# Attention and gated FFN on one core: two stages one after the other, and a woven layout with block transposes and column tiles

## The chip, the cores and the metric

One core of a Trainium2 chip runs one program. The metric is device time in microseconds (us). The kernel before was timed in three runs: 223.93, 224.61 and 225.66 us, median 224.61.

## The reference

q, k and v have the shape (batch 4, heads 4, tokens 1088, 32), in float32. S1 and S2 are 8 x 32.

```
phi(x)[i,j] = (S1 x)[i] * (S2 x)[j]              # 64 features of one token and head
kv  = sum over tokens of phi(k) (outer) v        # 64 x 32 for each batch and head
z   = sum over tokens of phi(k)                  # 64
att = phi(q) kv / (phi(q) . z + 1e-6)            # 32 for each token and head
x   = att, heads side by side                    # 4352 tokens x 128
out = (relu(x w_gate) * (x w_val)) w_out         # 128 -> 1536 -> 128
```

The order of work is set by the data: kv and z of a batch need all its keys, the attention of a token needs kv and z, and the FFN of a token needs its attention.

## The kernel before, in words

**Attention** goes through the four batches in a Python loop. The tokens of a batch are cut into eight chunks of 128 and one of 64, with a token on each partition. SyncE loads k and q, one DMA for each head plus one for the last 64 tokens, in runs of 128 bytes (32 floats); GpSimd loads v and casts it to 16 bits. For each chunk of k, TensorE transposes it (L135), VectorE copies the result from PSUM (L137), TensorE multiplies by s_bd, which holds S1 and S2 four times on the diagonal (L140), ScalarE copies (L142), GpSimd forms the outer products kp (L154), and TensorE adds kv (L158) and zbig, from which z comes (L144). After the nine chunks ScalarE places kv and z into two block matrices, kv_bd and the third part of s_bd_ext. The nine chunks of q then go the same way (transpose L183, matmul L188, outer product qp L195), and further: TensorE transposes qp (L202), VectorE copies (L208), TensorE multiplies by kv_bd (L211), GpSimd and VectorE form the denominator (L215 to L225), VectorE divides (L228), TensorE transposes the quotient (L236) and ScalarE writes it into xT, 128 features x 4352 tokens, 16 bits (L237).

**The FFN** starts when the attention's PSUM pools are closed: eight chunks of 512 tokens and one of 256. In a chunk each of the twelve slices j of the hidden width takes a matmul with w_gate (L250, g_ps), a relu on ScalarE (L252, g_sb), a matmul with w_val (L255, v_ps), and their product on VectorE (L256, ht); twelve accumulating matmuls with w_out follow (L260, ot_ps). ScalarE copies (L263), TensorE transposes four blocks (L272), ScalarE scales (L273), SyncE stores.

Every engine works through its own list in order. The lists are made by a list scheduler, which takes the instructions as the code issues them and orders them by its own costs and the free buffers of the pools; it can look ahead, so k of a batch overlaps with q of the batch before.

Of the kernel before, what the change touches and what calls it, by code (L numbers as in the profile page):

```python
# [9 lines left out]
BF16 = mybir.dt.bfloat16  # L11
FP16 = mybir.dt.float16
ALU = mybir.AluOpType
ACTF = mybir.ActivationFunctionType
XSCALE = 1.0 / 16.0


@with_exitstack
def kernel(
# [12 lines left out]
    nc = tc.nc  # L32
# [5 lines left out]
    NTOK = B * S  # L38
# [4 lines left out]
    SC = 128  # L43
    NCH = (S + SC - 1) // SC
    csz = [min(SC, S - i * SC) for i in range(NCH)]
    NFULL = S // SC
    CLAST = S - NFULL * SC
    HR = H * R

    const = ctx.enter_context(tc.tile_pool(name="const", bufs=1))  # L50
    xpool = ctx.enter_context(tc.tile_pool(name="xpool", bufs=1))
    a_in = ctx.enter_context(tc.tile_pool(name="a_in", bufs=2))
    a_tr = ctx.enter_context(tc.tile_pool(name="a_tr", bufs=5))
    a_ab = ctx.enter_context(tc.tile_pool(name="a_ab", bufs=5))
    a_kp = ctx.enter_context(tc.tile_pool(name="a_kp", bufs=5))
    a_qpt = ctx.enter_context(tc.tile_pool(name="a_qpt", bufs=5))
    a_sm = ctx.enter_context(tc.tile_pool(name="a_sm", bufs=6))
    a_pb = ctx.enter_context(tc.tile_pool(name="a_pb", bufs=2))
    f_h = ctx.enter_context(tc.tile_pool(name="f_h", bufs=2))
    f_g = ctx.enter_context(tc.tile_pool(name="f_g", bufs=4))  # L60
    f_o = ctx.enter_context(tc.tile_pool(name="f_o", bufs=4))


    ident = const.tile([128, 128], FP32)
    make_identity(nc, ident)
    ident16 = const.tile([128, 128], FP16)
    make_identity(nc, ident16)

    s_bd = const.tile([HD, 2 * HR], FP32)
    nc.vector.memset(s_bd, 0.0)  # L70
    for h in range(H):
        nc.scalar.dma_start(out=s_bd[h * D:(h + 1) * D, h * R:(h + 1) * R],
                            in_=S1.transpose([1, 0]))
        nc.scalar.dma_start(out=s_bd[h * D:(h + 1) * D, HR + h * R:HR + (h + 1) * R],
                            in_=S2.transpose([1, 0]))

    s1f = const.tile([HR, HD], FP32)
    nc.vector.memset(s1f, 0.0)
    for h in range(H):
        nc.scalar.dma_start(out=s1f[h * R:(h + 1) * R, h * D:(h + 1) * D], in_=S1)  # L80

    wg_sb = const.tile([DM, NJ, 128], FP16)
    nc.gpsimd.dma_start(out=wg_sb, in_=moe_w_gate.rearrange("m (j f) -> m j f", j=NJ))
    wv_sb = const.tile([DM, NJ, 128], FP16)
    nc.gpsimd.dma_start(out=wv_sb, in_=moe_w_val.rearrange("m (j f) -> m j f", j=NJ))
    wo_sb = const.tile([128, NJ, DM], FP16)
    nc.gpsimd.dma_start(out=wo_sb, in_=moe_w_out.rearrange("(j f) m -> f j m", f=128))

    xT = xpool.tile([HD, NTOK], FP16)

    with tc.tile_pool(name="ps_tr", bufs=2, space=bass.MemoryType.PSUM) as ps_tr, \
         tc.tile_pool(name="ps_xt", bufs=1, space=bass.MemoryType.PSUM) as ps_xt, \
         tc.tile_pool(name="ps_ab", bufs=1, space=bass.MemoryType.PSUM) as ps_ab, \
         tc.tile_pool(name="ps_kv0", bufs=1, space=bass.MemoryType.PSUM) as ps_kv0, \
         tc.tile_pool(name="ps_kv1", bufs=1, space=bass.MemoryType.PSUM) as ps_kv1, \
         tc.tile_pool(name="ps_zb", bufs=1, space=bass.MemoryType.PSUM) as ps_zb, \
         tc.tile_pool(name="ps_nd", bufs=1, space=bass.MemoryType.PSUM) as ps_nd:
        ab2_ps = ps_ab.tile([SC, 2, 96], FP32, name="ab2_ps")
        ndq2_ps = ps_nd.tile([SC, 512], FP32, name="ndq2_ps")
        xtsz_ps = ps_xt.tile([HD, 96], FP32, name="xtsz_ps")  # L100

        for b in range(B):
            q4 = a_in.tile([SC, NCH, H, D], FP32, name="q4")
            k4 = a_in.tile([SC, NCH, H, D], FP32, name="k4")
            v4 = a_in.tile([SC, NCH, H, D], FP16, name="v4")

            def load_qkv(dst, src, eng):
                for h in range(H):
                    eng.dma_start(
                        out=dst[:, 0:NFULL, h],  # L110
                        in_=src[b, h, 0:NFULL * SC, :].rearrange("(c p) d -> p c d", p=SC),
                    )
                eng.dma_start(
                    out=dst[:CLAST, NFULL],
                    in_=src[b, :, NFULL * SC:, :].transpose([1, 0, 2]),
                )

            load_qkv(k4, k, nc.sync)
            load_qkv(q4, q, nc.sync)
            load_qkv(v4, v, nc.gpsimd)  # L120

            kv_ps = [ps_kv0.tile([128, 2 * D], FP32, name="kv0_ps"),
                     ps_kv1.tile([128, 2 * D], FP32, name="kv1_ps")]
            zbig_ps = ps_zb.tile([HR, HR], FP32, name="zbig_ps")
            kv_bd = a_pb.tile([128, 2, F], FP16, name="kv_bd")
            s_bd_ext = a_pb.tile([HD, 3 * HR], FP32, name="s_bd_ext")
            zbig_sb = a_pb.tile([HR, HR], FP32, name="zbig_sb")

# [180 lines left out]
```

## Time and profile before

| what | value |
|---|---|
| median of three runs | 224.61 us (223.93 to 225.66) |
| span of the profiled execution, first to last instruction | 223.3 us |
| TensorE (PE) busy | 179.1 us, 80% |
| VectorE (DVE) busy | 106.2 us, 48% |
| ScalarE (ACT) busy | 103.2 us, 46% |
| GpSimd (POOL) busy | 82.1 us, 37% |
| first matmul of the attention | 14.2 us |
| first FFN matmul on the chain that ended last | 144.2 us |

The profiled execution's own time is known by its span alone: what lies around the first and the last instruction is not in the page, and the median of the runs is 1.3 us above that span. In the page, an engine's busy time is the union of its instructions. Matmuls are pipelined, so two matmuls that start 0.2 us apart may each be shown as 0.4 us long; the distance between their starts tells the pace. PEld is the loading of a matmul's stationary operand.

### The profile page before, as it was taken

The numbers are of one execution on the slowest core, as the hardware profiler recorded it, in microseconds if no ns is written. First come the engines' busy times: TensorE is split into PE (matmuls) and PEld (weight loads), VectorE is DVE, ScalarE is ACT, GpSimd is POOL, SyncE is SP. The second block draws the span as 40 slices with busy tenths as digits, with TensorE's granted clock in tenths as the row PEclk, the third lists the DMA queues.
The fourth block names the chain that finished last, engine by engine and source line by source line (L and its number), as shares of the span: only waits on it lengthen the run. The fifth ranks groups of instructions, "written<-read, shape, count | busy, mean of one in ns | idle before, by whom it ended". The sixth has DMA issues, their size and how long they took to land.

```text
span 223.3 us, 3087 instructions
## 1 busy us (share of the span) xinstructions
PE 179.1 (80%) x906; PEld 105.7 (47%) x906; DVE 106.2 (48%) x290; ACT 103.2 (46%) x307; POOL 82.1 (37%) x187
## 2 busy tenths in 40 slices
PE   0018999659949989689997795599999999999992
PEld 0005666437727667366674552234444444444460
DVE  0002003333114431224422154369998989989981
ACT  0021243112433213332234362158898988988981
POOL 8402578997378853158632385000000000000000
PEclk9999999999999999999999999559999999999998
DMA  7999989765494100000000000000110110110110
GB/s 95 156 125 135 156 107 84 72 23 44 72 52 72 28 0 0 3 0 1 0 1 3 0 0 1 0 0 3 47 48 0 47 51 0 47 42 6 50 47 23
DMA packets 61776, 9.18 MB, mean 41 GB/s; under 512 B 57152, under 2 KB 61504, under 8 KB 61760
## 3 DMA queue, kind: packets, MB, share of 16 engines
q1 hardware_dynamic: 39952, 6.69, 17.8%
q0 software_dynamic: 19568, 2.30, 17.0%
q10 hardware_dynamic: 2240, 0.01, 0.7%
q8 instruction: 7, 0.11, 0.2%
q14 instruction: 9, 0.07, 0.1%
HBM read 9.06 MB, written 2.23 MB: 51 GB/s over the span
## 4 chain that ended last, share of the span: by engine, by line
PE 60%; POOL 18%; DMA 7%; issue 5%; DVE 4%; ACT 4%; SPq 0%; ACTq 0%; POOLq 0%
PE v_ps L255 12%; PE ot_ps L260 10%; PE g_ps L250 10%; POOL qp L195 8%; PE ab_ps L140 7%; DMA k<-in_k_dram 4%; PE zbig_ps L144 4%; POOL den L223 3%; POOL bw L215 3%; PE tr_ps L183 3%; PE kv_ps L158 2%; DMA s_bd<-in_S_dram 2%; PE xtsz_ps L236 2%; PE ndq_ps L211 2%; PE ab_ps L188 2%
## 5 line engine op out<-in xcount | busy, mean ns | idle before, releaser
L256 DVE TENSOR_TENSOR ht<-g_sb,v_ps 128x512 f16<-128x512 f16 (+1 forms) x108 | 67.3, 656 | 8.1 <-PE v_ps L255 4.0
L252 ACT ACTIVATE g_sb<-g_ps 128x512 f16<-128x512 f32 (+1 forms) x108 | 59.1, 583 | 11.5 <-PE g_ps L250 7.9
L255 PE MATMUL v_ps<-xT,wv_sb 128*128 128x512 f16 (+1 forms) x108 | 40.7, 379 | 0.8 <-DVE ht L256 0.4
L250 PE MATMUL g_ps<-xT,wg_sb 128*128 128x512 f16 (+1 forms) x108 | 40.9, 382 | 0.0
L260 PE MATMUL ot_ps<-ht,wo_sb 128*128 128x512 f16 (+1 forms) x108 | 39.8, 374 | 0.2 <-DVE ht L256 0.2
L154 POOL TENSOR_TENSOR kp<-ab_sb 128x256 f16<-128x256 f32 (+1 forms) x36 | 22.2, 623 | 23.8 <-ACT ab_sb L142 20.6
L135 PE MATMUL tr_ps<-ident,k 128*128 128x128 f32 (+1 forms) x36 | 14.7, 435 | 17.8 <-DMA k<-in_k_dram 14.2
L188 PE MATMUL ab_ps<-s_bd_ext,tr_sb 128*128 128x96 f32 (+1 forms) x72 | 25.3, 455 | 4.5 <-ACT s_bd_ext L175 2.6
L195 POOL TENSOR_TENSOR qp<-ab_sb 128x256 f16<-128x256 f32 (+1 forms) x36 | 22.5, 625 | 13.1 <-ACT ab_sb L190 12.3
L142 ACT COPY ab_sb<-ab_ps 128x64 f32<-128x64 f32 (+1 forms) x36 | 7.6, 211 | 41.0 <-PE ab_ps L140 31.8
L140 PE MATMUL ab_ps<-s_bd,tr_sb 128*128 128x64 f32 (+1 forms) x72 | 23.5, 431 | 2.3 <-DMA s_bd<-in_S_dram 2.3
L188 PEld LDWEIGHTS ab_ps<-s_bd_ext,tr_sb 128*128 128x128 f32 (+1 forms) x72 | 17.1, 298 | 9.6 <-ACT ab_sb L190 5.4
L137 DVE COPY tr_sb<-tr_ps 128x128 f32<-128x128 f32 (+1 forms) x36 | 9.6, 275 | 25.4 <-PE tr_ps L135 21.9
L222 DVE TENSOR_REDUCE den<-bw 128x4 f32<-128x32 f32 (+1 forms) x36 | 6.6, 184 | 30.6 <-POOL bw L215 30.3
L190 ACT COPY ab_sb<-ab_ps 128x96 f32<-128x96 f32 (+1 forms) x36 | 8.6, 238 | 25.7 <-PE ab_ps L188 22.4
L140 PEld LDWEIGHTS ab_ps<-s_bd,tr_sb 128*128 128x128 f32 (+1 forms) x72 | 17.5, 305 | 4.7 <-issue 3.1
L208 DVE COPY qpt<-ndq_ps 128x256 f16<-128x256 f16 (+1 forms) x36 | 10.0, 277 | 17.8 <-PE ndq_ps L202 17.2
L135 PEld LDWEIGHTS tr_ps<-ident,k 128*128 128x128 f32 (+1 forms) x36 | 8.0, 229 | 20.9 <-issue 14.4
L250 PEld LDWEIGHTS <-wg_sb 128*128 128x128 f16 x108 | 11.1, 103 | 13.2 <-issue 4.7
L260 PEld LDWEIGHTS <-wo_sb 128*128 128x128 f16 x108 | 10.6, 98 | 14.1 <-issue 3.8
L255 PEld LDWEIGHTS <-wv_sb 128*128 128x128 f16 x108 | 10.7, 99 | 12.6 <-issue 2.9
L237 ACT COPY xT<-xtsz_ps 128x128 f16<-128x128 f16 (+1 forms) x36 | 9.4, 261 | 14.8 <-PE xtsz_ps L236 14.7
(44 smaller groups left out, 207.5 us busy)
## 6 DMA issues: line engine op xcount, KB each, us to landing
k<-in_k_dram SPq DMA_DIRECT2D x16, 128.0 KB, 3.5
q<-in_q_dram SPq DMA_DIRECT2D x16, 128.0 KB, 4.6
out_dram<-o_sb SPq DMA_DIRECT2D x8, 256.0 KB, 2.3
v<-in_v_dram POOLq DMA_DIRECT2D x16, 64.0 KB, 3.4
wg_sb<-in_moe_w_gate_dram POOLq DMA_DIRECT2D x1, 384.0 KB, 5.9
wv_sb<-in_moe_w_val_dram POOLq DMA_DIRECT2D x1, 384.0 KB, 7.5
wo_sb<-in_moe_w_out_dram POOLq DMA_DIRECT2D x1, 384.0 KB, 11.0
s_bd<-in_S_dram ACTq DMA_DIRECT2D x8, 1.0 KB, 5.6
```

Source lines behind the costliest of these rows:

```text
L135: nc.tensor.transpose(tr_ps[:, :c], k4[:c, ci].rearrange("s h d -> s (h d)"), ident[:c, :c])
L137: nc.vector.tensor_copy(out=tr_sb[:, :c], in_=tr_ps[:, :c])
L140: nc.tensor.matmul(ab_ps[:c, 0:2 * HR], tr_sb[:, :c], s_bd, start=True, stop=True)
L154: nc.gpsimd.tensor_tensor(out=kp[:c], in0=a_bc, in1=b_bc, op=ALU.mult)
L188: nc.tensor.matmul(ab_ps[:c], tr_sb[:, :c], s_bd_ext, start=True, stop=True)
L195: nc.gpsimd.tensor_tensor(out=qp[:c], in0=a_bc, in1=b_bc, op=ALU.mult)
L208: nc.vector.tensor_copy(out=qpt[:, :, :c], in_=qpt_ps[:, :, :c])
L250: nc.tensor.matmul(g_ps[:, :cs], wg_sb[:, j], xT[:, c0:c0 + cs], start=True, stop=True)
L252: nc.scalar.activation(out=g_sb[:, :cs], in_=g_ps[:, :cs], func=ACTF.Relu)
L255: nc.tensor.matmul(v_ps[:, :cs], wv_sb[:, j], xT[:, c0:c0 + cs], start=True, stop=True)
L256: nc.vector.tensor_tensor(out=ht[:, j, :cs], in0=g_sb[:, :cs], in1=v_ps[:, :cs], op=ALU.mult)
L260: nc.tensor.matmul(ot_ps[:, :cs], wo_sb[:, j], ht[:, j, :cs], start=(j == 0), stop=(j == NJ - 1))
```

## The change

The kernel function is written anew; the arithmetic stays the same, with the division moved from the quotient to one factor of phi(q).

- **Layout.** k and q are loaded so that partition 32h + t holds head h, and each run in memory is eight tokens of one head, 1 KB. v is loaded in runs of 1 KB too. VectorE transposes k and q in 32 x 32 blocks from SBUF to SBUF (kT, qT), in three pieces each for a batch.
- **Column tiles.** The matmuls by S1 and S2 have s_bd, 128 x 32 for each, as the stationary operand, and four groups of 32 tokens times 4 columns go to four quadrants of the output's partitions. VectorE turns the result back in 32 x 32 blocks (kab, qab).
- **Fewer, larger steps.** Outer products are made for two token columns at a time (512 elements per partition), the denominator for 512 tokens at a time, and the numerator comes out of TensorE already with the features on the partitions, so it is copied into xT with no transpose. The last 64 tokens of all four batches form one group, "rest".
- **Woven order.** A table gives each step a slot; a slot is one slice j of an FFN chunk. The table's order is the order in which the code issues the steps. Batch 0's attention comes first. Attention of batch b lies beside the two FFN chunks of batch b - 1 (chunks 0 and 1 for batch 0, and so on), and "rest" beside the seventh chunk. The list scheduler then orders each engine's list (MANUAL is False).
- **PSUM.** All pools are open all along: two banks for g_ps, two for v_ps, one for ot_ps, one for kv_ps, and two (ps_a) that are shared by all other results of the attention and by the FFN's last transposes.

The core of the new code:

```
+    def load_kq(src, b, name, engs):
+        dst = inp.tile([128, NBLK, D], FP32, name=name)
+        for h in range(H):
+            engs[h % len(engs)].dma_start(
+                out=dst[h * D:(h + 1) * D, 0:32].rearrange("t (g c) d -> t g (c d)", g=4),
+                in_=src[b, h, 0:SM, :].rearrange("(g t c) d -> t g (c d)", g=4, t=32),
+            )
...
+    def k_transpose(b, i):
...
+        a, e = ((0, 12), (12, 24), (24, 34))[i]
+        nc.vector.transpose(out=kT[b][:, a * 32:e * 32],
+                            in_=k4[b][:, a:e].rearrange("p c d -> p (c d)"))
...
+    def k_ab_mm(b, i):
...
+        for s in range(2):
+            for g in range(4):
+                nc.tensor.matmul(ps[32 * g:32 * g + 32, s * n:s * n + m], s_bd[:, s],
+                                 kT[b][:, c_cols(g, c0, min(c1, NC))], start=True, stop=True)
...
+    def k_kv(b, c):
...
+        for p in range(2):
+            nc.tensor.matmul(ps[:, p * 64:(p + 1) * 64].rearrange("p (h d) -> p h d", h=2),
+                             st["kp", b, c][:, p * 128:(p + 1) * 128],
+                             v4[b][:, 2 * p:2 * p + 2, c],
+                             start=(c == 0 and p == 0), stop=(c == NC), skip_group_check=True)
+        j = c % 4
+        nc.tensor.matmul(ps[32 * j:32 * j + 32, 128:160],
+                         ab[:, 0, o].rearrange("p h r -> p (h r)"),
+                         ab[:, 1, o].rearrange("p h r -> p (h r)"),
+                         start=False, stop=(c + 4 > NC), skip_group_check=True)
...
+    def q_mm(key):
...
+        for s in range(3):
+            for g in range(4):
+                nc.tensor.matmul(ps[32 * g:32 * g + 32, s * 128:(s + 1) * 128],
+                                 s_bd[:, s] if s < 2 else w_s[b],
+                                 qT[b][:, c_cols(g, 4 * i, 4 * i + 4)], start=True, stop=True)
...
+    def q_num(key):
...
+        for p in range(2):
+            nc.tensor.matmul(ps, kvbd[key[0]][:, p], t[:, p], start=(p == 0), stop=(p == 1))
...
+    plan_k(0, -30, True)
+    plan_q((0, 0), -12, True)
+    plan_q((0, 1), -8)
+    at(-14, kq_load, 1)
+    for b in range(1, B):
+        base = 2 * NJ * b
+        plan_k(b, base - 25)
+        plan_q((b, 0), base - 9)
+        plan_q((b, 1), base - 5)
+        if b + 1 < B:
+            at(base - 12, kq_load, b + 1)
+    plan_q("rest", 2 * NJ * (B - 1) + 3)
```

Inside the plans, k_transpose, k_ab_mm, k_ab_tr (back to kab), k_outer (kp), k_kv, k_fin (zs and kvbd), k_sz and k_sw (w_s) follow each other for k, and q_mm, q_tr (qab), q_bw, q_den, q_scale (a2), q_outer (qp), q_xpose, q_ev (qpt), q_num and q_x (xT) for q. In the steady part all outer products are GpSimd's; for batch 0 some are VectorE's.

How the lists of the engines changed, at three places. First, TensorE's list at the start, where the kernel before had one transpose (L183) and one matmul of 96 columns (L188) for each chunk of 128 tokens. Now two groups of 512 tokens (ps_a_280 is group (0, 0), ps_a_312 group (0, 1)) take twelve column tiles each, four quadrants times three factors; the line number is that of q_mm:

```order
L261 MATMUL kv_ps_231<-zs_259,s1f4_171 128x32
L285 MATMUL ps_a_280<-qT_0_152,s_bd_170 32x128 x2
L285 MATMUL ps_a_312<-qT_0_152,s_bd_170 32x128
L285 MATMUL ps_a_280<-qT_0_152,s_bd_170 32x128
L285 MATMUL ps_a_312<-qT_0_152,s_bd_170 32x128 x2
L285 MATMUL ps_a_280<-qT_0_152,s_bd_170 32x128 x5
L285 MATMUL ps_a_280<-qT_0_152,w_s0_177 32x128 x4
L285 MATMUL ps_a_312<-qT_0_152,s_bd_170 32x128 x5
L285 MATMUL ps_a_312<-qT_0_152,w_s0_177 32x128 x4
L337 LDWEIGHTS qp1_304
```

So the two groups' tiles stand mixed, the first group is complete after 16 of the 24 tiles, and neighbours in the list write to different quadrants.

Second, TensorE's list in the middle. In the kernel before, a stretch of the attention (batch 1's last numerators beside batch 2's k and the first transposes of its q) reads:

```order
L183 MATMUL tr_ps_1103<-ident_91,q4_906 128x128
L183 MATMUL tr_ps_1129<-ident_91,q4_906 128x128
L144 MATMUL zbig_ps_926<-ab_sb_1008 32x32
L211 LDWEIGHTS qpt_813
L211 MATMUL ndq2_ps_146<-kv_bd_548,qpt_813 128x64
```

In the changed kernel, the third slice of FFN chunk 1 reads so (v_ps_583 and g_ps_600 are FFN matmuls of that chunk, ot16_576 is the result of chunk 0, the rest is batch 1's attention):

```order
L379 LDWEIGHTS wv_sb_122
L379 MATMUL v_ps_583<-xT_176,wv_sb_122 128x512
L285 MATMUL ps_a_587<-qT_1_153,s_bd_170 32x128
L261 MATMUL kv_ps_463<-zs_571,s1f4_171 128x32
L285 MATMUL ps_a_587<-qT_1_153,s_bd_170 32x128 x3
L375 LDWEIGHTS wg_sb_120
L375 MATMUL g_ps_600<-xT_176,wg_sb_120 128x512
L407 LDWEIGHTS ot16_576
L407 MATMUL ps_a_606<-ident16_137,ot16_576 128x128
```

Attention of the next batch now stands between matmuls of the FFN, and the list changes between full matmuls and column tiles several times in a chunk.

Third, GpSimd's list at the start. Before, the outer products of batch 0's k (kp) and the next batch's v:

```order
L129 COPY s_bd_ext_170<-s_bd_101 128x64
L154 TENSOR_TENSOR kp_181<-ab_sb_178 128x256
L154 TENSOR_TENSOR kp_193<-ab_sb_190 128x256
L154 TENSOR_TENSOR kp_205<-ab_sb_202 128x256
L154 TENSOR_TENSOR kp_217<-ab_sb_214 128x256
L154 TENSOR_TENSOR kp_229<-ab_sb_226 128x256
```

Now (kp1 are batch 0's outer products of one column, the DMAs the loads of v for batches 1 to 3; bw, a2 and qp belong to the first q groups):

```order
L217 TENSOR_TENSOR kp1_220<-kab1_212 128x256
L90 DMA v4_1_111<-in_v_dram 128x4x256
L217 TENSOR_TENSOR kp1_226<-kab1_212 128x256
L94 DMA v4_1_111<-in_v_dram 64x4x32
L90 DMA v4_2_112<-in_v_dram 128x4x256
L94 DMA v4_2_112<-in_v_dram 64x4x32
L90 DMA v4_3_113<-in_v_dram 128x4x256
L94 DMA v4_3_113<-in_v_dram 64x4x32
L302 TENSOR_TENSOR bw_330<-qab_328 128x128
L319 TENSOR_TENSOR a2_341<-qab_328,rden_339 128x128
L217 TENSOR_TENSOR qp1_304<-a2_302,qab_293 128x256
L217 TENSOR_TENSOR qp2_343<-a2_341,qab_328 128x512
```

GpSimd has three outer products of batch 0's k instead of nine, all of v's loads are issued before the first q group, and one load stands ahead of the last kp.

More of the change, by code (lines that the diff above doesn't have):

```diff
@@ new lines, in ffn_mul, with ffn_out @@
+    def ffn_mul(n):
+        i, j = divmod(n, NJ)
+        cs = CH[i][1]
+        g_sb, v_ps = st.pop(("gv", n))
+        nc.vector.tensor_tensor(out=st["ht", i][:, j, :cs], in0=g_sb[:, :cs], in1=v_ps[:, :cs], op=ALU.mult)
+    def ffn_out(n):
+        i, j = divmod(n, NJ)
+        cs = CH[i][1]
+        if j == 0:
+            st["ot", i] = ps_o.tile([128, 512], FP32, name="ot_ps")
+        nc.tensor.matmul(st["ot", i][:, :cs], wo_sb[:, j], st["ht", i][:, j, :cs],
+                         start=(j == 0), stop=(j == NJ - 1))
```

541 lines of the change are left out of this document (343 added, 198 removed).

## The prediction

> **What bounds the kernel now.** The page's head and its slices come first.
>
> ```profile
> span 223.3 us, 3087 instructions
> PE   0018999659949989689997795599999999999992
> DVE  0002003333114431224422154369998989989981
> POOL 8402578997378853158632385000000000000000
> PE 60%; POOL 18%; DMA 7%; issue 5%; DVE 4%; ACT 4%; SPq 0%; ACTq 0%; POOLq 0%
> ```
>
> A slice is 5.6 us. For 25 slices POOL works and DVE is three tenths busy; then POOL is empty and DVE full. The last row, from the chain that ended last, says that PE sets the end, with POOL in second place. Two rows of that chain, taken in order of time, give a batch of attention, and three give the FFN's start and its pace:
>
> ```profile
> 95.48 0.76 PE ab_ps L188 x2
> 124.84 0.76 PE ab_ps L188 x2
> 144.18 0.60 PE v_ps L255
> 178.61 0.58 PE ot_ps L260 x2
> 187.15 0.58 PE ot_ps L260 x2
> ```
>
> The first q chunks of two batches stand 29.4 us apart. The FFN starts at 144.18, so it takes 223.3 - 144.2 = 79.1 us, and a chunk of 512 tokens takes 8.54 us. What fills a chunk, by the timeline of PE in its steady part and the groups by line:
>
> ```profile
> 160.91 0.38 PE L255 MATMUL v_ps<-xT,wv_sb 128*128 128x512 f16 x1
> 161.12 0.38 PE L260 MATMUL ot_ps<-ht,wo_sb 128*128 128x512 f16 x1
> 161.34 0.38 PE L250 MATMUL g_ps<-xT,wg_sb 128*128 128x512 f16 x1
> L256 DVE TENSOR_TENSOR ht<-g_sb,v_ps 128x512 f16<-128x512 f16 x96 | 62.5, 686 | 7.3 <-PE v_ps L255 3.7 <-ACT g_sb L252 2.4 <-PE g_ps L250 0.3
> L252 ACT ACTIVATE g_sb<-g_ps 128x512 f16<-128x512 f32 x96 | 55.0, 608 | 10.8 <-PE g_ps L250 7.2 <-DVE ht L256 2.1
> L273 ACT ACTIVATE o_sb<-ott_ps 128x512 f32<-128x512 f16 x8 | 5.0, 628 | 0.0
> L263 ACT CAST ot<-ot_ps 128x512 f16<-128x512 f32 x8 | 4.7, 582 | 0.0
> L272 PE MATMUL ott_ps<-ident,ot 128*128 128x128 f16 x34 | 3.4, 220 | 0.5 <-ACT ot L263 0.5
> ```
>
> Starts lie 0.215 us apart, so 36 matmuls take 7.8 us, and with four transposes PE needs 8.0 of the 8.54. DVE's union is 62.5/96 = 0.65 us a product, 7.8 a chunk. ACT needs 55.0/96 = 0.57 a relu, 6.9 a chunk, and 1.2 for two copies. So the FFN is nearly balanced and PE-led, while the attention, 144 of 223 us, leaves DVE and ACT mostly idle. The clock differs too:
>
> ```profile
> 100.00:120.00 20.00, 19.17 (x110) 13.78 (x109) 7.35 (x36) 5.74 (x28) 12.36 (x29) 1.00 0.01 2
> 140.00:150.00 10.00, 7.50 (x26) 2.87 (x26) 4.73 (x10) 3.55 (x8) 0.00 (x0) 0.50 0.00 0
> 99.61 0.31 PE L236 MATMUL xtsz_ps<-ident,x_sb 128*128 128x128 f16 x1
> 110.64 0.42 PE L202 MATMUL ndq_ps<-ident,qp 128*128 128x128 f16 x2
> 164.29 0.39 PE L272 MATMUL ott_ps<-ident,ot 128*128 128x128 f16 x4
> ```
>
> At 110 us two 16-bit transposes take 0.42 where one takes 0.31: 0.11 apart. At 164 us four take 0.39; with 0.22 for one (their mean) that is 0.057 apart. I therefore read the attention at half clock, although its window prints 1.00 (before 133 us the trace has no clock record); the row at 140 us shows a recorded half.
>
> **The change, term by term.** The time becomes: head (batch 0's attention), plus the FFN as it is now (79.1, its tail and its cold start included), plus what the woven attention adds on PE.
>
> *Head.* These rows carry it:
>
> ```profile
> 1.84 9.90 DMA k<-in_k_dram
> 19.14 2.97 SPq L109 DMA_DIRECT2D k<-in_k_dram  x4
> out_dram<-o_sb SPq DMA_DIRECT2D x8, 256.0 KB, 2.3
> L256 DVE TENSOR_TENSOR ht<-g_sb,v_ps 128x256 f16<-128x256 f16 x12 | 4.7, 419 | 0.8 <-PE v_ps L255 0.2
> 113.58 0.64 PE L183 MATMUL tr_ps<-ident,q 128*128 128x128 f32 x2
> L183 PE MATMUL tr_ps<-ident,q 128*128 128x128 f32 x32 | 12.9, 438 | 0.1
> L140 PE MATMUL ab_ps<-s_bd,tr_sb 128*128 128x64 f32 (+1 forms) x72 | 23.5, 431 | 2.3 <-DMA s_bd<-in_S_dram 2.3
> L154 POOL TENSOR_TENSOR kp<-ab_sb 128x256 f16<-128x256 f32 x32 | 19.8, 624 | 21.2 <-ACT ab_sb L142 18.0 <-PE kv_ps L158 2.8
> L215 POOL TENSOR_TENSOR bw<-ab_sb 128x32 f32<-128x32 f32 x32 | 8.0, 250 | 1.4
> L109 POOL DMA_DIRECT2D v<-in_v_dram x16 | 14.7, 931 | 0.8 <-PE xtsz_ps L236 0.8
> ```
>
> Batch 0's k landed at 11.7 us in 128-byte runs. Six issues at 2.97/4 = 0.74 put the last at 0.7 + 5 x 0.74 = 4.4; with the 2.3 of a store in longer runs k lands at 6.7 (11.7 is the other end). No block transpose is in this trace. Between DVE's 512 and 256 elements lie 1.04 ns each, which leaves 0.12 us fixed on 0.65; three pieces of 1088 elements make 1.5 us, and twice that if blocks went at half the pace. An fp32 pass of 128 columns takes 0.64 - 0.44 = 0.2 us at half clock, and a true fp32 matmul takes two passes (72 records for the 36 matmuls of L140).
>
> Whether tiles for different quadrants overlap is shown nowhere. One after the other, a tile costs 0.43; four abreast, 0.11. I take 0.21: one tile's second pass beside the next one's first, since the list keeps two passes of a tile together. Then: k at 6.7, transposed 8.2, S products 12.3 (4.1), last kp 15.1 (DVE's turn back 0.5, then on POOL kp 0.62, one v issue 0.93, kp 0.62), kv, z and w_s 16.5, q transposed 18.0, 24 q tiles 23.4, turned back 24.0, denominators 25.4. POOL then makes a2, qp1, qp2, qp1: by its 32 and 256 elements 1.68 ns each, so 0.41 + 0.62 + 1.06 + 0.62 = 2.7, to 28.1. Transposes, qpt (1024 elements, two ACT copies' worth), the numerator at half clock and xT: 0.4 + 1.1 + 1.0 + 0.6 = 3.1. **Head 31**, from 27 (abreast) to 40 (in series), and 5 more if k lands no sooner than before.
>
> *What is woven, per batch, on PE at full clock.* Column tiles: k has 8 x 288 columns and q 24 x 128, 5376 columns of two passes at 0.83 ns: 9.0 in series, 4.5 by my choice, 2.3 abreast. 18 kv matmuls and sixteen transposes, all with 128 loaded columns, at 0.057: 1.0 and 0.9. Four numerator matmuls at 0.215: 0.9. sz, one fp32 matmul: 0.4. Changes between full and narrow matmuls come to 9 for zbig and about 8 for the S groups. Their price:
>
> ```profile
> 109.34 0.46 PE L135 MATMUL tr_ps<-ident,k 128*128 128x128 f32 x1
> 109.80 0.32 PE L144 MATMUL zbig_ps<-ab_sb 128*32 128x32 f32 x2
> 110.05 0.69 PE L140 MATMUL ab_ps<-s_bd,tr_sb 128*128 128x64 f32 x2
> ```
>
> A 128 x 32 matmul started only when the transpose had ended, 0.46 after its start, where another transpose follows after 0.2; and 0.25 later PE was back at full width. I take 0.2 for each change in the fast part, nothing as the lower end: 17 x 0.2 = 3.4. The Trainium skill, TensorEngine Tiling (Array Packing), Key Properties, says that a change of tiling mode drains the engine, which speaks against weaving narrow matmuls between wide ones; the trace agrees, with 0.46 for 0.2. The Trainium skill, TensorE: Matmul & The Clock Gate, Measured speedup vs the span model, gives 2.38 times for three column tiles; by that page, as an estimate, 9.0 would become 3.8 and the sum 2 us less. No run here shows it.
>
> Sum 11.1 a batch (5.5 to 15.6 with both unknowns at their ends), 33.3 for three. "rest" adds 24 tiles of 32 columns and sixteen small matmuls, 3. PE's idle 0.5 in each of six chunks takes up 3.
>
> *What lies beside PE.* Two chunks and a batch ask PE for 16 + 11.1 = 27.1. DVE: 24 x 0.65 + 6.6 = 22.2, the latter by the same 0.12 and 1.04 ns (ten block transposes of 3520 elements in all 4.9, two denominators 1.1, kv, z and w_s 0.6). ACT: 13.8 + 2.4 + 3.4 = 20 (relu, the FFN's copies, qpt and xT). POOL: 4.5 kp and 4 qp at 1.06, bw and a2 at 0.41, so 10.6. So I cost their work and all later loads at nothing: PE covers it. Were block transposes twice as dear, DVE would need 26 and be level. On SP the loads of batch 3 stand ahead of stores whose buffers nobody needs soon.
>
> Sum: 31 + 79.1 + 33.3 + 3 - 3 = 143.4 as span; with the 1.3 us by which the median stands above the span, **145 us**.
>
> **The rivals.** *Tiles run abreast and changes are free.* For it: the tiles write disjoint quadrants and need no wait for each other. Against: the drain above. 27 + 79.1 + 3 x 5.5 + 2 - 3 + 1.3 = 123. DVE is then level: 62.5 + 4.7 + 3 x 6.6 + 1.1 = 88 from a head of 27, and 5 of tail, give 120.
>
> *Tiles run in series, or PE waits at the hand-overs.* For it: each fp32 matmul before was two passes of one tile. 40 + 79.1 + 3 x 15.6 + 4 - 3 + 1.3 = 168. The same follows if lists in fixed order make PE wait: a batch has some 17 places where PE's next instruction needs kp, zs, w_s, qab, qp, qpt or xT; behind it stand the FFN's next g_ps and v_ps, for which ACT and DVE wait in turn, and 0.5 us at each place adds 26. Before, two steps of q lay twice an outer product apart on the chain:
>
> ```profile
> 127.11 0.63 POOL qp L195
> 128.38 0.58 POOL qp L195
> ```
>
> *The clock stays at half, and the kernel is slower than before.* The rows at 100 us show half pace although PE was 19.2 of 20 us busy. If narrow fp32 matmuls and waits keep it so through the FFN, 288 matmuls cost twice their 0.215 (62 us more), the 256-wide ones 4, the woven work some 25: 145 + 90 = 235. It is slower than 225 only from about nine tenths of the FFN at half clock. Against: the FFN before rose to full pace 6 us after its start, and two thirds of the woven PE time is the same matmuls. The Trainium skill, TensorE: Matmul & The Clock Gate, Part 1, says that an idle window of some 3.4 us halves the clock; by that rule it would stay up here. The trace agrees as far as it shows just the two levels.
>
> That the list scheduler undoes the weave is excluded by its order: the first FFN matmul stands ahead of batch 1's first tile.
>
> **How the numbers follow.** Forecast (134 to 158): 0.51. Abreast (117 to 134): 0.25. Series or hand-overs (158 to 185): 0.17. Half clock for part of the FFN (185 to 222): 0.04; for nearly all: 0.02; within 1%, which is what timing this kernel can tell: 0.01. Leaving out the outer quarter of the one neighbour (0.06), the outer two fifths of the other (0.07) and the last three (0.07) gives a range of 121 to 174 us. Faster 0.97, same 0.01, slower 0.02.
>
> **What would show it.** The first g_ps at 27 to 40 us on the chain; starts of neighbouring column tiles 0.2 apart at half clock (0.4 in series, under 0.1 abreast); a pair of woven chunks every 27 us, plain ones still 8.5; PE above 90% and DVE near 80% from 31 us on; POOL no longer on the chain after the head; PEclk 1.00 beyond 40 us. The prediction is wrong if PE's waits before kv, xpose and xT matmuls exceed 10 us in sum, if k lands after 10 us, or if the clock falls back in the weave.

## The result, and the profile after

The changed kernel takes **152.16 us** (median of four runs, 151.39 to 153.29) against 224.9 for the kernel before in the same comparison (four runs, 223.93 to 225.66): a ratio of 0.6763, 95% interval 0.6723 to 0.6802. The forecast was 145 us, the range 121 to 174. The profiled execution took 151.67 us with a span of 149.9; the sum of the prediction was 143.4 as span, so 6.5 us are to be explained, and, since errors can cancel, the terms as well.

First the head of the page after, with the same rows as before: busy times, slices (now 3.75 us each), and the chain's shares by engine.

```profile
span 149.9 us, 2886 instructions
PE 120.5 (80%) x1038; PEld 61.7 (41%) x1038; DVE 100.2 (67%) x213; ACT 82.1 (55%) x146; POOL 51.5 (34%) x75
PE   0035966269999998799999879999998899999950
DVE  4133754905968688698798685867788386889840
PEclk9999999758999999999999999999999999999996
PE 63%; POOL 9%; DVE 8%; DMA 6%; issue 4%; ACT 3%; SPq 2%; POOLq 1%; DVEq 0%; ACTq 0%
```

From the tenth slice on PE stands at nine tenths in most of them, beside a DVE at 50 to 90%; the 25 slices of half-empty attention are gone. POOL's share of the chain fell from 18 to 9%.

Now the chain in order of time: the head, the FFN's start, and the first w_out matmuls of chunks 0, 2, 4 and 7.

```profile
3.69 8.77 DMA k<-in_k_dram
13.12 1.08 PE ps_a L201 x11
21.85 3.12 PE ps_a L285 x48
33.39 0.43 PE g_ps L375
37.71 0.43 PE ot_ps L393 x2
66.43 0.43 PE ot_ps L393 x2
94.39 0.43 PE ot_ps L393 x2
131.91 0.43 PE ot_ps L393 x2
```

The head ends at 33.4 instead of 31. Two pairs of woven chunks take 28.7 and 28.0 us (forecast 27.1); the third pair and the chunk with "rest" together 37.5 (forecast 27.1 + 11.5 = 38.6); chunk 7, the last chunk and the tail 18.0 (forecast 8.5 + 10.8 = 19.3). The 4.3 us from the first g_ps to 37.71 are not all surplus: the kernel before has such a start too, between its first FFN matmul on the chain (144.18) and this one.

```profile
146.13 0.43 PE ot_ps L260
```

These 1.95 us lie in the forecast's 79.1 and so in its 19.3, which leaves 17.4 for the end. Set against the forecast, the head took 2.4 us more, the start of the FFN 2.4, the two pairs 2.5 and the end 0.6, while the third pair with "rest" took 1.1 less: 6.8 together, since these rounded parts of the forecast add to 143.1.

What a woven stretch looks like on TensorE, in the timeline of its second pair:

```profile
63.26 0.65 PE L201 MATMUL ps_a<-kT,s_bd 128*32 128x128 f32 x16
63.84 0.39 PE L375 MATMUL g_ps<-xT,wg_sb 128*128 128x512 f16 x1
71.58 0.38 PE L379 MATMUL v_ps<-xT,wv_sb 128*128 128x512 f16 x1
71.89 0.25 PE L242 MATMUL kv_ps<-kab 128*32 128x32 f32 x2
72.07 0.39 PE L393 MATMUL ot_ps<-ht,wo_sb 128*128 128x512 f16 x1
```

Eight column tiles (16 passes) are past in 63.84 - 63.26 = 0.58 us, the two changes included; at the prediction's prices they are 1.7 in series, 0.85 by its choice and 0.43 abreast. A lone zbig between two wide matmuls needs 72.07 - 71.58 = 0.49 where a wide matmul needs 0.215, so 0.28 for two narrow passes and two changes.

### The profile page after: what moved, and what is told of

Same layout as the page of the kernel before. It is cut to its first block, busy times and chain, and to the rows that moved or that the text cites. A ratio compares the mean times of both kernels' runs of the same rounds, so it can differ in the third digit from the quotient of the medians.

```text
span 149.9 us, 2886 instructions
## 1 busy us (share of the span) xinstructions
PE 120.5 (80%) x1038; PEld 61.7 (41%) x1038; DVE 100.2 (67%) x213; ACT 82.1 (55%) x146; POOL 51.5 (34%) x75
## 3 DMA queue, kind: packets, MB, share of 16 engines
q1 hardware_dynamic: 8032, 6.62, 17.4%
q0 software_dynamic: 5040, 2.29, 13.1%
## 4 chain that ended last, share of the span: by engine, by line
PE 63%; POOL 9%; DVE 8%; DMA 6%; issue 4%; ACT 3%; SPq 2%; POOLq 1%; DVEq 0%; ACTq 0%
PE g_ps L375 14%; PE v_ps L379 13%; PE ot_ps L393 13%; POOL qp L217 7%; DMA k<-in_k_dram 6%; PE ps_a L285 6%; PE kv_ps L242 5%; DVE ht L386 4%; PE ps_a L337 3%; PE ps_a L201 3%; PE kv_ps L237 3%; POOL a L319 2%; PE ps_a L358 2%; ACT g_sb L377 2%; PE ps_a L407 1%
## 5 line engine op out<-in xcount | busy, mean ns | idle before, releaser
L217 POOL TENSOR_TENSOR kp<-kab 128x512 f16<-128x512 f32 (+1 forms) x18 | 17.2, 976 | 22.9 <-DVE kab L212 19.2
L343 ACT COPY qpt<-ps_a 128x1024 f16<-128x1024 f16 (+1 forms) x9 | 8.7, 963 | 27.9 <-PE ps_a L337 27.9
L217 POOL TENSOR_TENSOR qp<-a,qab 128x512 f16<-128x512 f32 (+2 forms) x18 | 18.3, 1037 | 0.5
L201 PE MATMUL ps_a<-kT,s_bd 128*32 128x128 f32 x128 | 7.2, 314 | 12.0 <-DVE s_bd L158 8.2
L337 PE MATMUL ps_a<-ident,qp 128*128 128x128 f16 (+1 forms) x72 | 9.6, 238 | 8.4 <-POOL qp L217 8.4
L379 PEld LDWEIGHTS <-wv_sb 128*128 128x128 f16 x108 | 10.6, 98 | 9.6 <-issue 3.4
L375 PEld LDWEIGHTS <-wg_sb 128*128 128x128 f16 x108 | 10.6, 98 | 8.6 <-issue 2.1
L285 PE MATMUL ps_a<-qT,s_bd 128*32 128x128 f32 x128 | 9.8, 314 | 0.9 <-DVE qT L188 0.9
L242 PE MATMUL kv_ps<-kab 128*32 128x32 f32 x72 | 9.6, 218 | 0.0
L181 DVE STREAM_TRANSPOSE kT<-k 128x384 f32<-128x384 f32 (+1 forms) x12 | 6.3, 536 | 4.3 <-DMA k<-in_k_dram 4.3
L237 PE MATMUL kv_ps<-v,kp 128*128 128x64 f16 x72 | 8.8, 204 | 0.2 <-DVE kp L217 0.2
L237 PEld LDWEIGHTS <-kp 128*128 128x128 f16 x72 | 6.2, 101 | 5.9 <-DVE kp L217 0.3
```

The lines of the kernel that those rows point to most:

```text
L201: nc.tensor.matmul(ps[32 * g:32 * g + 32, s * n:s * n + m], s_bd[:, s], kT[b][:, c_cols(g, c0, min(c1, NC))], start=True, stop=True)
L217: eng.tensor_tensor(out=dst.rearrange("p c (h i j) -> p (c h) i j", h=H, i=R), in0=a.rearrange("p c h i -> p (c h) i")[:, :, :, None].to_b ...
L237: nc.tensor.matmul(ps[:, p * 64:(p + 1) * 64].rearrange("p (h d) -> p h d", h=2), st["kp", b, c][:, p * 128:(p + 1) * 128], v4[b][:, 2 * p ...
L242: nc.tensor.matmul(ps[32 * j:32 * j + 32, 128:160], ab[:, 0, o].rearrange("p h r -> p (h r)"), ab[:, 1, o].rearrange("p h r -> p (h r)"), ...
L285: nc.tensor.matmul(ps[32 * g:32 * g + 32, s * 128:(s + 1) * 128], s_bd[:, s] if s < 2 else w_s[b], qT[b][:, c_cols(g, 4 * i, 4 * i + 4)], ...
L337: nc.tensor.transpose(st["qpt", key][:, p, c * n:(c + 1) * n], st["qp", key, c][0:n, p * 128:(p + 1) * 128], ident16[0:n, 0:n])
```

## The experiments

All ratios are to the kernel before in the same comparison (225.5 to 226.5 us), with 95% intervals; the changed kernel's 0.6763 is 152.8 us on that scale, and 0.01 is 2.3 us.

**The landing of k: three runs.** In the changed kernel k's third block transpose started at 12.55 us, after a wait of 3.9. First the small pieces were issued ahead:

```
     def load_kq(src, b, name, engs):
+        for g in range(2):      # tokens 1024.. first
+            engs[...].dma_start(out=dst[:, 32 + g], ...)
         for h in range(H):
             engs[...].dma_start(out=dst[h * D:(h + 1) * D, 0:32], ...)
-        for g in range(2):
-            engs[...].dma_start(out=dst[:, 32 + g], ...)
```

> The loads of k and q are issued with the two 16 KB pieces (tokens 1024 to 1087, runs of 128 bytes) ahead of the four large ones. In the changed kernel the two first block transposes started at 7.48 us, when the large pieces were there, and the third waited for the small pieces until 12.55. Theory A (the small pieces come late because they are issued last and then share the DMA engines with the weights, v and q): they land early, the last block transpose of k starts by about 9 us, the first g_ps by about 30 us instead of 33.2, and the time falls by 3 to 4 us, to 148 to 149. Rival B (runs of 128 bytes are slow wherever they stand): the large pieces now wait behind them, k is complete no sooner than 12 us, and the time stays at 152.

Measured: 154.37 us, ratio 0.6818 (0.6791 to 0.6846), some 1 us slower; the two intervals just overlap. Then the weights were held back, by a write that each weight's DMA must wait for:

```
+    for w in (wg_sb, wv_sb, wo_sb):
+        nc.gpsimd.tensor_copy(out=w[:, 0, 0:34], in_=k4[0][:, 0:34, 0])
     nc.gpsimd.dma_start(out=wg_sb, ...)
```

> The DMAs of the three FFN weights wait until batch 0's k is complete: GpSimd first copies a few elements of k into each weight tile, which the DMA then overwrites. Theory A (k waits for the weights' traffic on the shared DMA engines): k is complete at 8 to 9 us, the first g_ps comes at 29 to 30, and the time falls by 3 to 4 us, to 148 to 149; the weights then land at about 25 us, ahead of their use. Rival B (the small runs of k are slow by themselves, or wait for something else): k is complete at 12.5 as before, the time stays at 152, or rises if the weights land after 33 us.

Measured: 151.43 us, ratio 0.6679 (0.664 to 0.6718): 2 us gained by the ratio. The two profiled executions, with spans of 149.7 and 149.9 us, differ by only 0.2, so the size is uncertain. And last, with zbig grouped as below, everything else of the start waits for k:

```
+    for t in v4:
+        nc.gpsimd.tensor_copy(out=t[:, 0, 0], in_=k4[0][:, 2:34, 0])
+        nc.gpsimd.tensor_copy(out=t[0:SL, 0, NC], in_=k4[0][0:SL, 2:34, 0])
...
+        nc.gpsimd.tensor_copy(out=q4[0][:, 0:34, 0], in_=k4[0][:, 0:34, 0])
```

> zbig grouped, and behind batch 0's k wait not only the weights but also batch 0's q and all of v (GpSimd writes a few elements of k into each of these tiles, which the DMA overwrites). It is to show when k is complete with the DMA engines to itself. If the rest of its delay (9.7 us with the weights held back) is traffic of v and q, the last block transpose of k starts at 6.5 to 7.5 us, as the prediction's 6.7 would have it; if it is the 128-byte runs or the issue on SyncE's queue, at 9 us or later. The time is not expected to be better than that of the run before: v and q land later, by some 4 us, and kv or the q tiles wait for them; 145 to 149 us.

Measured: 144.44 us, ratio 0.6399 (0.6373 to 0.6425), against 0.6336 (0.6311 to 0.6361) with the weights alone held back. VectorE's timeline shows k's last block transpose; the bracket is the wait ahead of it. In the changed kernel:

```profile
12.55 0.51 DVE L181 STREAM_TRANSPOSE kT<-k 128x320 f32<-128x320 f32 x1 [3.90 <-DMA k<-in_k_dram]
```

With the small pieces first, all three transposes of k in one row:

```profile
12.99 1.43 DVE L181 STREAM_TRANSPOSE kT<-k 128x384 f32<-128x384 f32 x3 [8.32 <-DMA k<-in_k_dram]
```

With late weights:

```profile
9.72 0.51 DVE L183 STREAM_TRANSPOSE kT<-k 128x320 f32<-128x320 f32 x1 [1.18 <-DMA k<-in_k_dram]
```

With k alone, again three in one row:

```profile
5.32 1.43 DVE L188 STREAM_TRANSPOSE kT<-k 128x384 f32<-128x384 f32 x3 [0.36 <-DMA k<-in_k_dram]
```

With the DMA engines to itself k is there, small runs and all, when the three pieces follow each other from 5.3 us on, so the last of them starts at 6.3 (a row of 1.43 for three). The weights cost k 2.8 us, and v and q some 3.5 more. The order of k's own pieces only decides which of them meets that traffic: expectation A of the first run was wrong. A of the second was right in the cause, and at most about half of its gain came. In the third the traffic of v and q was the answer, but what the early k won was lost again: TensorE waited 2.9 us for v and 3.8 for qT, and the first g_ps came at 34.1 against 30.2.

**Grouped zbig.** The nine zbig matmuls of a batch stand together behind the last kv pair:

```
-        j = c % 4
-        nc.tensor.matmul(ps[32 * j:32 * j + 32, 128:160], ...)
+        if c < NC:
+            return
+        for c in range(NC + 1):
+            ...
+            nc.tensor.matmul(ps[32 * j:32 * j + 32, 128:160], ...)
```

> The nine zbig matmuls of a batch (32 loaded columns, for z) are issued together behind the last kv pair, so that TensorE changes between full and column tiles two or three times for them in place of nine. Theory A (a change costs: 0.28 us for a lone zbig with its two changes at full clock in the changed kernel, 0.47 for a zbig and a kv pair at half clock in the head): eight of nine lose about 0.2 us, 1.6 for each of three woven batches and 2 to 3 in the head, so 148 to 150 us. Rival B (the 0.28 is two fp32 passes, and no change has a price): the time stays within 1 us of 152, and neighbouring zbig matmuls stand 0.2 apart. Rival C (z comes later and the wait for zs moves onto the chain): 152 to 154.

Measured: 147.8 us, ratio 0.6527 (0.6488 to 0.6565): **5.3 us** gained, as theory A said, but none of it in the head, whose first g_ps comes at 33.7 us. The busy times in its page:

```profile
PE 114.4 (78%) x1038; PEld 57.3 (39%) x1038; DVE 99.7 (68%) x213; ACT 81.5 (56%) x146; POOL 51.4 (35%) x75
```

The groups by line and shape, zbig here (two passes for each of 36 matmuls; busy us, mean ns) and in the changed kernel:

```profile
L246 PE MATMUL kv_ps<-kab 128*32 128x32 f32 x72 | 2.1, 213 | 0.0
```
```profile
L242 PE MATMUL kv_ps<-kab 128*32 128x32 f32 x72 | 9.6, 218 | 0.0
```

And the timeline here, with all nine of a batch in one row:

```profile
73.17 0.38 PE L246 MATMUL kv_ps<-kab 128*32 128x32 f32 x18
73.48 0.39 PE L397 MATMUL ot_ps<-ht,wo_sb 128*128 128x512 f16 x1
```

From the first start to the next wide matmul nine take 73.48 - 73.17 = 0.31 us, and one alone took 72.07 - 71.89 = 0.18 above. By the order of the lists TensorE changes 123 times between full and column tiles in the changed kernel and 61 times here; PE's busy time fell by 6.1 us, so **0.10 for a change**. Behind the first g_ps alone the price is the same: 56 changes in place of 102, and 4.5 us less of busy time.

**Column tiles quadrant by quadrant.**

```
         for s in range(2):
-            for g in range(4):
-                nc.tensor.matmul(ps[32 * g:..., ...)
+        for g in range(4):
+            for s in range(2):
+                nc.tensor.matmul(ps[32 * g:..., ...)      # q_mm alike, with range(3)
```

> The column tiles by S1, S2 and w_s are issued quadrant by quadrant, so that a tile's neighbours write to the same quadrant (before: four quadrants in turn). The work is the same. Theory A (four tiles run at the same time because they stand in different quadrants): neighbours in one quadrant follow one another, a pass of 128 columns each 0.055 us apart at full clock; 5376 columns of two passes then take 4.5 to 9 us of TensorE per batch in place of 2.3, so the time rises by 2 to 6 us for each of three woven batches and by 2 to 6 in the head: 160 to 175 us. Rival B (the overlap is the usual pipelining of short matmuls, whatever their quadrant): starts lie as close as before, 152 us within 1.

Measured: 160.32 us, ratio 0.7095 (0.7067 to 0.7123), 7.5 us more. Pieces of the chain, here and in the changed kernel:

```profile
55.15 1.28 PE ps_a L285 x20
```
```profile
110.10 0.79 PE ps_a L285 x22
```

So a pass costs 0.064 in this order and 0.036 in the changed kernel's. Theory A holds: tiles overlap because their neighbours use other quadrants. The size is at the lower end, probably since the last tile of one quadrant still overlaps with the first of the next; this was not measured by itself.

**No weave.**

```
-        base = 2 * NJ * b
+        base = 30 * (b - B)
...
+    at(-0.5, gate)      # w[:, :, 0] = 0 * xT[:, last 12 columns] + w[:, :, 0]
```

> All attention ahead of the FFN: the attention of batches 1 to 3 and the rest group get earlier slots, and VectorE adds zero times the last columns of xT to the first column of each slice of w_gate and w_val (12 values per partition), so that no FFN matmul can start before the attention ends. Layout, column tiles and block transposes stay. Theory A (most of the gain is the layout's, and the weave hides only what TensorE waits for): a batch without FFN is bound by its own chain of hand-overs and GpSimd's 10.6 us, some 15 to 18 us each; 33 + 3 x 16 + 3 + 79 = 163, from 157 to 172. Rival B (the weave carries the gain: a batch alone takes as long as the head of 27 us from k's landing): 33 + 3 x 27 + 3 + 79 = 196, from 185 to 205. The clock is likely to be halved in the attention.

Measured: 194.77 us, ratio 0.8601 (0.8558 to 0.8643). On its chain, the q tiles of three of the four batches and the FFN's start:

```profile
21.75 3.54 PE ps_a L285 x48
45.16 3.54 PE ps_a L285 x48
91.26 3.48 PE ps_a L285 x48
113.44 0.61 PE g_ps L375
```

The busy times of PE, PEld, DVE, ACT and POOL in the stretch of one batch:

```profile
45.20:68.20 23.00, 14.79 (x156) 10.17 (x157) 6.74 (x20) 3.20 (x4) 10.61 (x13) 1.00 0.10 25
```

Rival B was right. A batch alone takes 23.0 us, at half pace (48 passes in 3.5 us) and with no engine full. The 1.00 in the row is no measurement: this trace has no clock record before 84 us, and the q tiles at 91.26, where the record says half, take as long as those before. The same batch beside two chunks costs 28.0 - 2 x 8.5 = 11. Of the 73 us between the two kernels the new layout alone brings 32 (1 - 0.8601 of 226) and the weave 41. Part of the 41 is the clock: the batch keeps PE busy for 14.8 us alone, and in the second woven pair, as shown further down, for 26.4 - 16 = 10.4.

**The table's order, without the list scheduler.** The edit is MANUAL = True.

> The list scheduler is off (MANUAL is True): every engine works in the order of the table. TensorE's list then has 101 changes between full and column tiles in place of 123. Theory A (a change costs about 0.1 us, and the rest of the order matters little): 2 us less, 149 to 151. Rival B (the table issues a step when its slot comes, whether its input is there or not, and TensorE's waits for qp, qpt and kT grow): 155 to 165.

Measured: 165.35 us, ratio 0.7313 (0.7276 to 0.735), 12 us slower. The waits of the FFN's relu and product, here and in the changed kernel (us in total, times, longest):

```profile
ACT g_sb L377 <- PE g_ps L375: 39.7, 59, 2.4
DVE ht L386 <- ACT g_sb L377: 36.7, 46, 5.6
```
```profile
ACT g_sb L377 <- PE g_ps L375: 23.7, 39, 1.4
DVE ht L386 <- ACT g_sb L377: 15.5, 23, 5.2
```

PE stands at a step of the attention whose input is not there yet, and the FFN behind it waits: behind the first g_ps PE's own waits sum to 15.7 us here and 5.1 in the changed kernel. The 22 changes less are lost in that. The clock's record also falls to half once, from 70.7 to 74.1 us.

**The hand-over of qp: two runs.** In the first, half of the outer products goes to VectorE:

```
             at(s + 2, q_outer, key, 0, 2, G)
-            at(s + 3.5, q_outer, key, 2, 4, G)
+            at(s + 2, q_outer, key, 2, 4, V)
```

> Of the two outer products qp of every group of q after the first, the second goes to VectorE instead of GpSimd. Theory A (the hand-over from GpSimd is on TensorE's path: in the changed kernel PE waited 8.4 us for qp in 11 places, and the chain has 1.08 of GpSimd twice per group): TensorE's wait for qp falls below 4 us, VectorE's work rises by 8 x 0.7 = 5.6 us and still has room, and the time falls by 3 to 5 us, to 147 to 149. Rival B (VectorE's products of the FFN come later by what it takes over, since its list is in order): the wait moves from qp to ht, and the time stays within 1 us of 152.

Measured: 154.84 us, ratio 0.6848 (0.682 to 0.6876), 1.9 us **slower**; TensorE's wait for qp went from 8.4 to 9.5 us in sum. Both theories missed it. Its timeline where both engines make a product of the same group:

```profile
62.07 0.69 DVE L217 TENSOR_TENSOR qp<-a,qab 128x512 f16<-128x512 f32 x1
62.11 1.57 POOL L217 TENSOR_TENSOR qp<-a,qab 128x512 f16<-128x512 f32 x1
```

POOL's group of such products here and in the changed kernel (busy us, mean ns):

```profile
L217 POOL TENSOR_TENSOR qp<-a,qab 128x512 f16<-128x512 f32 x7 | 9.7, 1382 | 0.5
```
```profile
L217 POOL TENSOR_TENSOR qp<-a,qab 128x512 f16<-128x512 f32 x14 | 14.9, 1080 | 0.5
```

The two products start 0.04 us apart, and POOL's takes 1.57 us; five of the seven did. In the changed kernel DVE is as busy beside POOL, but with ht, which reads one of its two inputs from PSUM, and two of POOL's products take no more than 2.09:

```profile
83.42 2.09 POOL L217 TENSOR_TENSOR qp<-a,qab 128x512 f16<-128x512 f32 x2
83.82 1.34 DVE L386 TENSOR_TENSOR ht<-g_sb,v_ps 128x512 f16<-128x512 f16 x2 [0.35 <-PE g_ps L375]
```

So a product on DVE with both inputs in SBUF costs POOL 0.5 us. The Trainium skill, SBUF — State Buffer, Who interferes with whom, says that VectorE's two-input operation from SBUF contends with GpSimd's reads; the trace agrees. This is not the whole loss: the list also has 131 changes of form in place of 123, and the first g_ps comes at 34.6 us in place of 33.4. How the 1.9 us divide is not shown.

In the second, on top of grouped zbig and late weights, the woven attention starts three slots earlier, and the steps from q_xpose on keep their slots:

```
-        plan_k(b, base - 25)
-        plan_q((b, 0), base - 9)
-        plan_q((b, 1), base - 5)
+        plan_k(b, base - 28)
+        plan_q((b, 0), base - 12, late=3)
+        plan_q((b, 1), base - 8, late=3)
```

> The version with grouped zbig and late weights, and in the table the woven attention of batches 1 to 3 starts three slots earlier, while the transposes of qp and what follows keep their slots: qp has three slots (some 3 us) more before TensorE's list comes to it. Theory A (TensorE's waits for qp in the weave, 4.1 us behind the head in the version without, are a question of the list's order): they fall below 1.5 us, and the time falls by 2 to 3 us, to 140.5 to 141.5. Rival B (the list scheduler has its own costs, in which qp was ready in time, so that the slots change little; or another wait takes its place, for VectorE's ht or a ps_a buffer that is held longer): 143 to 144, within 1 us.

Measured: 142.6 us, ratio 0.6311 (0.6285 to 0.6337). TensorE's waits behind the head, in the version without (from 34 us on) and with it:

```profile
PE ps_a L343 <- POOL qp L219: 4.1, 9, 0.9
```
```profile
PE v_ps L385 <- DVE ht L392: 1.7, 4, 0.7
PE ps_a L343 <- POOL qp L219: 0.2, 1, 0.2
```

The wait is gone, yet the ratio fell by 0.0025 only, 0.6 us, and the intervals overlap: not the 2 to 3 us of theory A. A wait for ht came in its place (1.7 us), and the new order has 67 changes between tile forms in place of 61. Rival B stands, in its second form.

**A warm clock for the head: two runs.**

```
+    nc.vector.memset(hot, 0.0)
+    for i in range(NWARM):      # 40, then 24
+        wps = ps_g.tile([128, 512], FP32, name="g_ps")
+        nc.tensor.matmul(wps, hot[:, 0:128], hot, start=True, stop=True)
```

> Forty matmuls of zeros, 128 x 512 in 16 bits, run on TensorE from about 1.5 us, before k has landed; nothing reads their result. Theory A (the head runs at half clock because TensorE idled before it): the clock is up from about 5 us, and the head's TensorE steps on the chain (S products 1.1, kv and zbig 4.3, q tiles 3.1) take half to two thirds as long if the clock stays up over the wait for k; the first g_ps comes 2 to 4 us sooner, 148 to 150 us. Rival B (the head waits for VectorE, GpSimd and DMA, or the clock falls again in the gap before k at 12.5 us): within 1 us of 152.

Measured: 155.35 us, ratio 0.6853 (0.6801 to 0.6905), 2 us slower; the two intervals just touch. The forty matmuls started late, since VectorE wrote their zeros only at 6.4 us, and they kept k's tiles waiting; the timeline has them in one row:

```profile
6.72 11.53 PE L174 MATMUL g_ps<-hot 128*128 128x512 f16 x40 [6.72 <-DVE hot L171]
```

From the first S product to the first g_ps it then took 36.1 - 18.2 = 17.9 us, against 33.4 - 13.1 = 20.3. The clock's record is at full from 12.2 to 29.3 us here; one stretch of it, with the end of kv and most of the q tiles:

```profile
22.74:26.15 3.41, 3.10 (x53) 2.12 (x52) 1.19 (x5) 0.00 (x0) 0.21 (x1) 1.00 0.77 142
```

A kv pair with its zbig took 0.34 us in place of 0.47, and from the first S product to the last q tile it took 7.7 us in place of 11.9. Not all of that need be the clock, since v and q had landed by then. Of the 4.2 us 1.8 were lost again behind the q tiles, and k's tiles had waited 5.1 us for the zeros to end. The second try, on top of grouped zbig and late weights:

> zbig grouped, weights held back, and 24 matmuls of zeros (128 x 512, 16 bits) on TensorE from about 1 us, their input written first of all on VectorE; in the earlier run they started at 6.7 us, since the input came late, and ended at 18.2, over 5 us after k. Now they should end at 9 to 9.5, as k lands at 9.7. Theory A (TensorE's steps of the head then run at full clock: 0.34 in place of 0.47 for a kv pair with zbig, 1.2 for all S products, 2 for the q tiles in place of 3.5): the first g_ps comes 2 to 3 us sooner than without, 142 to 143 us. Rival B (the waits of the head, 1 to 3 us each, let the clock fall before the q tiles, or VectorE and GpSimd set the pace): within 1 us of the version without.

Measured: 143.36 us, ratio 0.6343 (0.6319 to 0.6367), the same as without. Its zeros in the timeline:

```profile
1.25 7.58 PE L104 MATMUL g_ps<-hot 128*128 128x512 f16 x24 [1.25 <-DVE warm L139]
```

Its q tiles on the chain, and those of the version without:

```profile
17.63 3.58 PE ps_a L297 x48
```
```profile
18.21 3.58 PE ps_a L291 x48
```

And three stretches of it, cut where the clock's records change (PE's busy time comes first, the granted clock third from the end):

```profile
9.20:12.61 3.41, 1.69 (x46) 1.25 (x40) 2.20 (x5) 0.00 (x0) 2.92 (x8) 1.00 1.10 190
12.61:16.02 3.41, 1.43 (x18) 0.88 (x19) 1.93 (x3) 0.00 (x0) 3.40 (x6) 0.50 1.09 190
16.02:19.43 3.41, 2.93 (x51) 2.68 (x54) 1.82 (x6) 0.00 (x0) 2.42 (x4) 0.50 1.52 205
```

After one stretch in which PE was busy for half the time the clock was at half again, before most of kv; a stretch with 2.93 of 3.41 did not bring it back. So rival B holds for the second try: the gaps behind k's landing lost the clock. The first try shows the other side: where PE had no such gaps the clock stayed at full through the q tiles. Zeros that also fill the gaps, without keeping k's tiles waiting, were not tried.

**The edits that won, together.** Grouped zbig and late weights:

> The two edits that won are put together: the nine zbig matmuls of a batch issued behind the last kv pair, and the weights' DMAs held back until batch 0's k is complete. If the two gains are separate (mode changes in the weave, 5 us; k's landing, 2 us), they add to a ratio of 0.6763 - 0.0236 - 0.0084 = 0.644 of the kernel before, 145 us. If the head's gain of grouping was the same as that of the earlier k (in the run with grouped zbig TensorE waited for q in the head, by the chain), the ratio is 0.650 or more.

Measured: **143.35 us**, ratio 0.6336 (0.6311 to 0.6361). The sum of the two gains would have been 0.644, so they more than add. The head shows part of it: grouping alone leaves the first g_ps at 33.7, late weights bring it to 31.9, both to 30.2, since with grouping alone q's transposes still started at 21.0 us, as late as in the changed kernel (21.1), when q had landed. The rest of the head's gain depends on when the clock rises: its records reach full at 37.3, 35.9 and 32.2 us in the three traces (34.6 in the changed kernel), and the first w_out matmul comes at 39.1, 37.5 and 34.9 (37.7). One trace of each cannot tell how much of that is chance, so why the gains more than add stays open. With the three slots of slack, 142.6 us is the shortest time measured.

## Why the prediction was right, and where its terms were not

- **What bounds it.** Right: PE is full in the weave, and PE, not DVE, sets the pace. The run without the weave shows that the half-empty engines were the resource.
- **k's landing.** Wrong: the step put k at 6.7 us, transposed at 8.2, with 5 more as the other end; the transposes ended at 13.1, at that other end. With the DMA engines to itself k was there no later than the step had it; what failed is that the weights', v's and q's traffic was left out of this term. That k lands after 10 us was named as a sign that the prediction is wrong, and it came.
- **The rest of the head and the tile choice.** From the transposes to the first g_ps it took 33.4 - 13.1 = 20.3 us, not 31 - 8.2 = 22.8: the middle price for tiles was too dear. 24 of them took 3.12 us, 0.13 each, against 0.21 taken and 0.11 abreast. The S products took 2.1 in place of 4.1, too. Against that, from the end of the S products to w_s it took 5.9 us (15.2 to 21.1) in place of 4.2, since the nine kv pairs with their zbig stand 0.47 us apart. Together this hid half of k's error, which is luck. In the weave the tiles were mis-sized as well: 84 passes a batch at 0.036 are 3.0 us, not 4.5.
- **Mode changes.** 17 x 0.2 = 3.4 a batch came out right. The step counts nine for nine zbig, so one for the way to the narrow form and back; by single changes there are 102 behind the first g_ps, 34 for each of three batches (those of "rest" among them), at 0.10 each. The size is in part luck: 0.2 was chosen between nothing and one row at half pace, whose way in alone cost 0.46 - 0.2 = 0.26.
- **The head's end.** The step counted one q group behind POOL's products. The second group's eight transposes come ahead of the first g_ps, while the first group's xT is made, but its numerator comes behind it. It is part of the 4.3 us before 37.71, as are batch 1's first column tiles, which the sum counts with the woven work, and FFN matmuls at half clock, which the kernel before has at its start as well.
- **Hand-overs.** The rival with 0.5 us at each of 17 places, 26 us, did not come. TensorE's waits behind the head, in the changed kernel:

```profile
PE ps_a L337 <- POOL qp L217: 4.1, 9, 0.9
```

Nine places with 0.45 each: the price was right, but the rival has 17 places in each of three batches, 51 in all. The sum itself has nothing for them; in the second woven pair PE is idle for 1.7 of 28.1 us, and busy for 26.4 where the sum has 27.1. And the table's order shows that the rival is real once the lists are not sorted: 12 us.
- **What would show it.** Right: pairs near 27, PEclk full beyond 40 us, and PE above 90% in the woven pairs; the second one, by its stretch (PE, PEld, DVE, ACT, POOL):

```profile
61.90:90.00 28.10, 26.43 (x237) 12.99 (x235) 22.95 (x46) 18.95 (x33) 10.79 (x14) 1.00 0.14 42
```

PE has 94%, DVE 82%, and DVE's 23.0, ACT's 19.0 and POOL's 10.8 stand beside the forecast 22.2, 20 and 10.6. PE's waits before kv and xpose matmuls sum to 8.6 us, below the 10 that would have shown it wrong (10.0 with the 1.4 for qpt). Wrong: that POOL leaves the chain after the head. This piece of it stands there in the first woven batch, and the like in the others:

```profile
55.46 2.10 POOL qp L217 x2
```

- **Clock at half.** It did not come in the weave (the row above has 1.00); the run with all attention ahead shows that the attention by itself stays at half pace.

## What to carry to other kernels

Give a stage that leaves every engine half empty to a neighbour that fills one: here a batch of attention cost 23 us alone and 11 beside the FFN, and that was more than the new layout brought. Count the changes between matmul forms in the order that the scheduler really made, and put narrow matmuls together: that was 5 us for a few lines. At the start, list every DMA that shares the engines with the first operand, and hold back those that nobody needs soon.

## What the runs showed of the hardware that was not expected

- Passes of 128 columns into four quadrants in turn cost 0.036 us each, in the other order 0.064; a change of form cost 0.10. The Trainium skill, TensorE: Matmul & The Clock Gate, Measured speedup vs the span model, has 2.38 for three column tiles; these runs have no order without any overlap, so they show only that the ratio here is at least 1.8.
- GpSimd's 512-element product takes 1.57 in place of 1.08 us when VectorE makes its own from SBUF at the same time; beside VectorE's ht, with one input in PSUM, two take 2.09.
- The clock fell to half after a stretch of 3.41 us in which PE was busy for 1.69. The Trainium skill, TensorE: Matmul & The Clock Gate, Part 1, speaks of an idle window of some 3.4 us; the trace agrees with the window's length, but here a window that was half idle was enough. Busy time alone does not decide: 2.93 of 3.41 us did not bring the clock back there, while in the changed kernel the clock's records begin, at full, behind a stretch with 2.54 (20.98 to 24.39 us).
